# Three more input slots in the space of X2, a buffer of its own for the small spectra, and a smaller identity: one change to a fused recurrence and FFT-convolution kernel

## The chip, the cores and the metric

The kernel runs on one core of a Trainium2 chip. A core has four engines that compute: PE (matrix multiply, with its weight loads shown as PEld), DVE, ACT and POOL. SP issues the DMAs. Only PE writes to PSUM, and only DVE and ACT read it here. The metric is the device time of one execution in microseconds (us). Lower is better. For the kernel before, three executions gave 456.35, 457.14 and 457.5 us.

## The reference

The input x has 4 batches of 6272 time steps with 256 channels. First comes a gated linear recurrence, then a gated convolution over the whole sequence, computed with FFTs, between two projections.

```python
sig = 1.0 / (1.0 + np.exp(-f_logit))
f = lower_bound + (1.0 - lower_bound) * sig          # i = 1 - f
for t in range(S):
    h = f[:, t] * h + i[:, t] * x[:, t]
    y[:, t] = h
proj = y @ w_proj                                     # 256 -> 3 * 256: x1, x2, x3
X2 = np.fft.rfft(x2, n=S, axis=1)
H = np.fft.rfft(filter_fft, n=S, axis=0)
x2_conv = np.fft.irfft(X2 * H, n=S, axis=1)
out = (x1 * x2_conv * x3) @ w_out
```

## The kernel before

Every batch passes through the same phases.

- hgrn(b) computes the recurrence in 13 chunks of 512 steps (the last has 128). Of each chunk f_logit and x are loaded into a slot (FL and XT, L331). ACT takes the sigmoid in place (L334), POOL multiplies x by it (L336), and PE transposes both by 64x64 blocks against an identity matrix (L348, "su"). ACT or DVE makes f of it (L361, L363), and DVE runs the scan (L369), which writes h into HA. The two halves of the channels (kh) are done one after the other, so a chunk has two "su" and two scans. For the first six chunks there is also a copy behind the end of the sequence ("wrap").
- phase_p(b) projects h onto x2 by columns of HA with a step of 49 elements (98 matmuls with 256 columns, L703), and ACT or DVE moves the result from PSUM into X2 (L280, L285). It needs the whole scan of the batch.
- The spectrum runs in 16 units of 8 pairs. phase_f1 takes X2 as weights (L716), the result goes to A. "mini" and "zm" (L732, L737) multiply the real end frequencies of four units by the small spectra Hm and leave the products in zp. unit does the second step of the transform (L778), multiplies by the filter's spectrum H, which is loaded from DRAM again for most units (L756). That product is made by DVE straight from PSUM (L801), or by an evacuation to A and a product on POOL (L810). POOL adds the two halves of zp into PP ("slot", L783). I2 is the first step back (L820); its result goes to Th.
- gate(b) computes x1 times x3 in 13 chunks (L397 with L282, L287, L418, L427).
- phase_o(b) does the last step back (L883), multiplies by the gate on DVE (L889), projects by w_out (L901), evacuates and stores (L913).

In the prologue, the filter is loaded and transformed by the same two steps (L633, L651), the tables are made, and the H spectra are stored to DRAM. X2 serves there as a place for raw filter rows, and in batch 0 for three input slots more (more, slots0). Later the input has NX = 3 slots, which chunks take in turn by count["x"].

X2 holds, for each of 128 pairs, a row of PW = 116 elements: 49 columns, 15 of zeros, 49 columns, and 3 more of zeros. Hm, the small spectra, stands in 8 of those 15 columns of zeros (xv[:, :, Q:Q + 8]). "pad" (L665, L670) writes the zeros once, after the scan of batch 0.

What runs in which order is written by hand into a table, ORDER: for each operation its number, its engine and its PSUM bank. The operations are first declared with what they read and write (r, w), and the table is then issued in its sequence, so that every engine gets its instructions in this order and works them off one after the other. SP is a queue of this kind too: a load that waits for its slot holds up everything issued behind it. The operations of hgrn(b+1) stand in the table among those of the spectrum, gate(b) and phase_o(b).

Where an operation may run on either engine, the table chooses. "MUL" stands for a product made by DVE straight from PSUM.

Of the kernel before, what the change touches and what calls it, by code (L numbers as in the profile page):

```python
# [45 lines left out]
PW = 116  # L46
PF = 113
NX2 = 13
WR = 3072
# [12 lines left out]
class Plan:  # L62
# [63 lines left out]
    "A3gA7gAzgA/gAAYAOYAVIA0YA4AAhQAcQABIACIAPIASYAQAAWIAjQAaQAbQAdQAfQAgQAeQA5QA1SAoUBAYAiUA2KA8ABHgBfgBPgAlUBBUArWAnWBD"  # L126
    "gBLgBXgBTgBbgBjgA9WAsSA6ABIYBJSBCMBEYAyAARAAYUAwVDqgDrgDngAkVD2gECgADgD3gDpgEOgDogEDgEPgEagAqVBQIA+OAXIBFQAmVBRWAuVB"
    "SGApVBGAAZEBKKBYIAUIBMYBNSATYBUYAxVBZWBgABOKBaOAtVBVQBWABcIAvUBhWBiOBdUBkYBeEBlQBmIBpUBqMBwQBxIBnWBoODsAD4ADtYEEAB3U"
    "BuQBvIBrYAEYByYBsWBtOB4EDuSBzQB+UB0AB5WD5YDyQB/EB6GCAUEQACBEDvKDwKB7YEFYCCYB8SDzID0ID6WB9CCDUCEED+QCJSCQUD/AEcAEmgD7"
    "OD8OERYEbgCKKCRMCOWEAIEngEygEGSCHUCIMCPGEHCEIKEoAEdYCLYCSYEKWCTQELGCMUCUACNEEMOESSCZQETKCXWE0AEWUCaICYGCeQCgWEUKE8gE"  # L130
    "zgAFgE9gFGgFQgCGgEpYEJYCbYEXMEYME+ACfAChGCcSCdCEeQEiWEjGEfIEgICnUCoECpSEqUEkOAIACqCCjQCwSCuWErECiYE1YAJYCkAEsMEuQFIA"
    "CvGCsUCxKE2SCzWEvIEwICtEC+UC0GE3KE4KE5QCrYAHYAKYCyYC/EE/YE6ADAWE7IDBGC3UFASC5WFSAC4EDDQC6GFDUDEAC8WC9GEhYFHgFbgF6gFJ"
    "YCVgFRgCmgC7YFTYDCYFagCFgFkgFlgB2gFugCWgDGgFvgAGgFcAFBKFCKFKSDJQJTWJUXFEMFFMFLKDKAJWHJVODOUDPEFmAFMKDHQFNWDIAJYUFOOF"
    "POJaEFUSDQQFVCDRADMUFWKFXWFdYDNEFwAFnYDLYEtYALYDSYAMYEVYElYFxYDXQFYOFZOFeSDYADTUFfCFhQDUEDZWFgKFiADaGFjIFoUFpEDeSDfC"
    "DgWDhGFrQFySDcWFqMJZUJdVFzKF0KF1SFsAMugB1gC2gF4gGlgG3gF/gDWgClgDFgMigMWgF5gC1gMXgD1YEBYExYJXYANYDxYD9YDbYF7YF8YDiYFt"
    "IF2KF3KDdGDjWJbsJeQJiRENAEZAJfFGHSGTUJkBJgoDkOGVQGJWGWIGICMwAGUEGKOGXSGFQGZUGYCGGIGaEMkAGBWGRSGDUGSCGLQGNSGCOMYAGEMG"
    "MIGOKGPUGQEJjWJnXJoQJluJpHJqoGbUDmgDlgHAgMjgDVgGugGdSGhWGcEGeKGfQGmUJsSGiGGgAGosGqsF9WJuCJtTHTgHJQJxSJvrF+GGjUJzCGvW"
# [55 lines left out]
def kernel(  # L193
# [124 lines left out]
    def hgrn(b):  # L318
        for c in range(NCHK):
# [665 lines left out]
```

## Time and profile before

| | |
|---|---|
| median of 3 executions | 457.14 us |
| the profiled execution | 457.66 us, its span 455.5 us |
| PE busy | 436.8 us (96%) |
| DVE busy | 407.9 us (90%) |
| ACT busy | 392.8 us (86%) |
| POOL busy | 307.6 us (68%) |
| read from and written to HBM | 86.12 MB and 31.98 MB |

The span is the time from the first to the last record of the profiled execution. The busy time of PE counts matmuls whose ends are modelled, one overlapping the next, so a PE that is busy need not be at its peak. A row of a group gives line, engine, operation, output and inputs, shape, count, then the busy time in us and the mean duration of one in ns, and after the second bar the idle time of the engine ahead of these instructions with what ended it. A row of the chain of work gives its start and its length in us, and what the chain stood in. A row "A <- B: 31.7, 12, 12.5" of the waits says that A waited for B for 31.7 us in 12 times, and 12.5 us the longest time.

### The profile page before, as it was taken

What the parts mean: (1) busy time and instruction counts of PE and PEld (TensorE: products, weight loads), DVE (VectorE), ACT (ScalarE), POOL (GpSimd) and SP (SyncE); (2) the same over time, 40 slices, a digit from 0 to 9 for tenths busy, and PEclk for the clock granted to TensorE, in tenths of its full rate; (3) what the DMA queues carried; (4) which work ended last, traced back from release to release, by engine and by line L of the source; (5) the groups of instructions that cost most, each with busy time, mean ns of one, the idle gap of its engine ahead of it and who ended that gap; (6) DMA issues with size and microseconds to landing.
All of it is one profiled execution on the core that took longest, in us unless ns stands there. A gap on an engine that the chain in (4) does not pass through costs nothing.

```text
span 455.5 us, 14537 instructions
## 1 busy us (share of the span) xinstructions
PE 436.8 (96%) x6017; PEld 344.1 (76%) x6017; DVE 407.9 (90%) x456; ACT 392.8 (86%) x545; POOL 307.6 (68%) x287
## 2 busy tenths in 40 slices
PE   8999999999999999999999999999999899999994
PEld 6877778667767889767768988776769797776783
DVE  5889998899999986999999987999999859988973
ACT  5789998889999988999988978999999778998354
POOL 4588994289998642889986626999996505657300
PEclk9999999999999999999999999999999999999999
DMA  8999979767797977559956893589586822763167
GB/s 326 406 402 380 373 254 362 275 217 242 273 322 237 333 250 316 173 172 325 357 195 232 308 358 146 179 293 339 192 309 210 349 115 89 219 199 111 47 266 302
DMA packets 42562, 119.04 MB, mean 261 GB/s; under 512 B 4096, under 2 KB 5760, under 8 KB 42496
## 3 DMA queue, kind: packets, MB, share of 16 engines
q1 hardware_dynamic: 42496, 118.11, 72.7%
q8 instruction: 47, 0.77, 0.7%
q14 instruction: 19, 0.16, 0.1%
HBM read 86.12 MB, written 31.98 MB: 259 GB/s over the span
## 4 chain that ended last, share of the span: by engine, by line
PE 58%; DVE 14%; ACT 8%; issue 5%; DMA 5%; POOL 3%; SPq 0%; DVEq 0%; ACTq 0%; POOLq 0%
PE PS L397 14%; PE PS L820 8%; PE PS L703 7%; PE PS L901 7%; DVE HA L369 6%; PE PS L348 6%; PE PS L716 5%; PE PS L778 5%; DMA FL<-in_f_logit_dram 3%; PE PS L883 3%; DVE ys L889 3%; DMA XT<-in_x_dram 2%; DVE fTs L363 2%; PE PS L633 2%; DVE PP L801 2%
## 5 line engine op out<-in xcount | busy, mean ns | idle before, releaser
L336 POOL TENSOR_TENSOR XT<-XT,FL 128x1024 f32<-128x1024 f32 (+1 forms) x47 | 105.1, 2239 | 59.5 <-ACT FL L334 31.7
L369 DVE TENSOR_TENSOR_SCAN HA<-fTs,HA,PS 128x512 f16<-128x512 f32 (+1 forms) x96 | 112.8, 1204 | 3.0 <-ACT fTs L361 2.2
L397 PE MATMUL PS<-HA,W 128*128 128x490 f16 (+1 forms) x416 | 100.4, 367 | 0.3 <-ACT XS L282 0.2
L810 POOL TENSOR_TENSOR PP<-HA,Hu 98x1008 f16<-98x1008 f16 x43 | 90.2, 2106 | 4.3 <-ACT HA L280 2.0
L280 ACT CAST HA<-PS 128x1024 f16<-128x1024 f32 (+1 forms) x106 | 83.5, 821 | 4.9 <-PE PS L716 1.8
L889 DVE TENSOR_TENSOR ys<-PS,zt 128x1024 fp32r<-128x1024 f32 (+1 forms) x52 | 58.5, 1153 | 9.7 <-PE PS L883 5.4
L801 DVE TENSOR_TENSOR PP<-PS,Hu 98x1008 f16<-98x1008 f32 x53 | 62.2, 1199 | 1.5 <-PE PS L820 0.7
L901 PE MATMUL PS<-Wo,ys 128*128 128x256 f32 x392 | 57.8, 293 | 3.3 <-DVE ys L889 2.6
L361 ACT ACTIVATE fTs<-PS,nomc 128x512 f32<-128x512 f32 (+1 forms) x84 | 55.8, 673 | 4.7 <-PE PS L348 2.3
L397 PEld LDWEIGHTS <-W 128*128 128x128 f16 x416 | 35.2, 97 | 29.9 <-issue 3.3
L820 PEld LDWEIGHTS <-PP 98*128 98x128 f16 x1024 | 48.9, 98 | 11.3 <-issue 2.9
L418 DVE TENSOR_TENSOR zt<-PS,XS 128x490 f16<-128x490 f32 (+1 forms) x86 | 54.7, 653 | 2.3 <-DVE XS L287 0.5
L282 ACT ACTIVATE XS<-PS 128x490 f32<-128x490 f32 (+1 forms) x85 | 49.0, 584 | 8.7 <-DVE zt L418 5.1
L901 PEld LDWEIGHTS PS<-Wo,ys 128*128 128x128 f32 x392 | 49.5, 188 | 8.3 <-ACT PP L282 1.5
L280 ACT CAST Th<-PS 128x784 f16<-128x784 f32 x63 | 51.7, 823 | 4.0 <-PE PS L820 3.3
L820 PE MATMUL PS<-VA,PP 98*128 98x98 f16 x512 | 52.0, 207 | 0.8 <-POOL PP L783 0.3
L820 PE MATMUL PS<-VB,PP 98*128 98x98 f16 x512 | 51.8, 207 | 0.0
L334 ACT ACTIVATE FL<-FL 128x1024 f32<-128x1024 f32 (+1 forms) x47 | 47.4, 1012 | 3.0 <-DMA FL<-in_f_logit_dram 2.8
L703 PE MATMUL PS<-W,HA 128*128 128x256 f16 x392 | 43.8, 273 | 0.0
L703 PEld LDWEIGHTS <-HA 128*128 128x128 f16 x392 | 42.8, 142 | 0.7 <-ACT XS L282 0.3
L348 PE MATMUL PS<-iden,FL 64*128 64x64 f32 x704 | 40.3, 230 | 2.7 <-ACT osb L282 1.4
L348 PEld LDWEIGHTS PS<-iden,FL 64*128 64x128 f32 x704 | 30.2, 138 | 15.1 <-DVE HA L369 3.4
(112 smaller groups left out, 764.8 us busy)
## 6 DMA issues: line engine op xcount, KB each, us to landing
FL<-in_f_logit_dram SPq DMA_DIRECT2D x43, 512.0 KB, 5.9
XT<-in_x_dram SPq DMA_DIRECT2D x43, 512.0 KB, 6.7
Hu<-H SPq DMA_DIRECT2D x39, 512.0 KB, 4.4
out_dram<-osb SPq DMA_DIRECT2D x24, 512.0 KB, 4.6
out_dram<-PP SPq DMA_DIRECT2D x16, 512.0 KB, 5.2
Hl<-H SPq DMA_DIRECT2D x13, 512.0 KB, 4.5
out_dram<-HA SPq DMA_DIRECT2D x8, 512.0 KB, 6.1
X<-in_moe_filter_fft_dram SPq DMA_DIRECT2D x7, 512.0 KB, 6.2
```

The lines of the kernel that those rows point to most:

```text
L280: nc.scalar.copy(dst, src)
L336: op("u", {"POOL": 0.1 + 0.553 * nb}, lambda e, xt=xt, ft=ft: nc.gpsimd.tensor_tensor(xt, xt, ft, op=AOP.mult), r=[("ft", k)], w=[("xt", k)])
L348: nc.tensor.transpose(bank(pb)[:, at[p] + j:at[p] + hn:nb], src[ps, j, cols], iden[ps, ps])
L361: nc.scalar.activation(fT, sT, AF.Identity, scale=by, bias=1.0)
L369: nc.vector.tensor_tensor_scan(h, fT, bank(pb)[:, 512 - hn:512 + hn], init, op0=AOP.mult, op1=AOP.add),
L397: nc.tensor.matmul(PS[:, p, 0:n], W13[:, kh, js], HA[:, HB[kh] + t0:HB[kh] + t0 + n], start=(kh == 0), stop=(kh == 1))
L703: nc.tensor.matmul(pp[:, r - r0, :], column(HB[kh], q_of(r)), W2[:, kh, :], start=(kh == 0), stop=(kh == 1))
L801: nc.vector.tensor_tensor(pr, px.unsqueeze(1).broadcast_to([TB, 2, UE, 63]), hh(), op=AOP.mult)
L810: nc.gpsimd.tensor_tensor(pr, spec[:, o, :, 1:64].unsqueeze(1).broadcast_to([TB, 2, UE, 63]), hh(), op=AOP.mult)
L820: nc.tensor.matmul(PS[:, ib + o, pr * TB:(pr + 1) * TB], PP[:TB, k, o, n, 2 * pr:2 * pr + 2, :], v[:TB], start=(n == 0), stop=(n == 1))
L889: nc.vector.tensor_tensor(late["ys"][:, yk, :, 0:rn * 128], PS[:, cb:cb + 2, 0:rn * 128], late["zt"][:].rearrange("p k r m -> p k (r m)") ...
L901: nc.tensor.matmul(po[:, i, :], late["ys"][:, yk, kh, i * 128:(i + 1) * 128], Wo[:, kh, :], start=(kh == 0), stop=(kh == 1))
```

## The change

X2 is lent to the input again in batches 1 to 3. LENT names the chunks of a batch that use the three slots in X2; the others take the three normal slots in turn. lend() is an operation without an instruction that puts the borrowed use behind the last reader of X2 and the next use of X2 behind the borrowed one. Since the input overwrites the zeros, pads() writes them again after every scan (a memset of 15 columns in each row and one of the end, on POOL). Hm can no longer stand in the zeros and gets a buffer of its own, in which the 128 pairs lie side by side. The room for it comes from several places: rows of X2 are 113 elements and not 116, the tables FT, VA and VB lie in one buffer at a distance of 98 elements, zp has one buffer and not two, XS is shorter, and the identity that stays is [128, 64] (two 64x64 blocks one above the other). The full identity is f16 and lives only in the prologue. ORDER is new as a whole.

```diff
-PW = 116
+PW = 113
+LENT = ((), (5, 6, 7, 8, 9, 10), (5, 6, 7, 8, 9, 10), (7, 8, 9, 10))
...
-    iden = konst.tile([128, 128], F32, name="iden")
+    idc = konst.tile([128, 64], F32, name="idc")
...
-    FT = konst.tile([128, 2, 2, 128], F16, name="FT")
-    VA = konst.tile([128, TB], F16, name="VA")
-    VB = konst.tile([128, TB], F16, name="VB")
+    FTf = konst.tile([128, 6 * TB], F16, name="FT")
+    def FT(rows, o, r):
+        return FTf[rows, (2 * o + r) * TB:(2 * o + r) * TB + 128]
+    VA, VB = FTf[:, 4 * TB:5 * TB], FTf[:, 5 * TB:6 * TB]
...
-    Hm = xv[:, :, Q:Q + 8].rearrange("m i (e a k) -> m e a k i", e=2, a=2)
+    Hmt = konst.tile([128, 2, 2, 2, NEP], F16, name="Hm")
+    Hm = Hmt[:]
...
-    zp = konst.tile([128, 2, 2, 2, 2, NA * UE], F16, name="zp")
+    zp = konst.tile([128, 2, 2, 2, NA * UE], F16, name="zp")
...
+    count["x"] = 2
+    x2t = [("raw", i) for i in range(7)] + [("x2", g) for g in range(NX2)] + ["padX"]
+    x2t += [(t, NX + i) for t in ("ft", "xt") for i in range(3)]
+    def lend():
+        op("pre", {"SP": 0.01}, lambda e: None, w=x2t)
+    def pads():
+        op("pad", {"POOL": 2.0}, lambda e: nc.gpsimd.memset(xv[:, :, Q:64], 0.0), w=["padX"])
+        def tails(e):
+            nc.gpsimd.memset(X2[:, NEP * PW:], 0.0)
+        op("pad", {"POOL": 0.6}, tails, w=["padX"])
...
             if b == 0:
                 k = slots0[c]
+            elif c in LENT[b]:
+                k = NX + LENT[b].index(c) % 3
             else:
                 k = count["x"] % NX
...
-                                                    src[ps, j, cols], iden[ps, ps])
+                                                    src[ps, j, cols], idc[ps])
...
+        iden = tmp.tile([128, 128], F16, name="iden")
         op("iden", {"POOL": 0.6}, lambda e: make_identity(nc, iden), w=["iden"])
+        def corners(e):
+            for i in range(2):
+                at = slice(64 * i, 64 * i + 64)
+                dve.tensor_copy(idc[at], iden[at, at])
+        op("idc", {"DVE": 0.2}, corners, r=["iden"], w=["idc"])
...
-                e, xv[:TB, :, Q:Q + 8].rearrange("p i (e c) -> p i e c", e=2),
-                PS[:TB, pb:pb + 2].rearrange("p e (c i) -> p i e c", c=4), HS),
+                e, Hmt[:TB].rearrange("p e a k i -> p e (a k i)"), PS[:TB, pb:pb + 2], HS),
...
-        op("zm", {"DVE": 0.58}, prod, r=["Hm"], w=[("zp", q % 2)], src=mm)
+        op("zm", {"DVE": 0.58}, prod, r=["Hm"], w=["zp"], src=mm)
...
             if b + 1 < B:
                 plan.batch = b + 1
+                lend()
                 hgrn(b + 1)
+                lend()
+                pads()
```

More of the change, by code (lines that the diff above doesn't have):

```diff
@@ new lines @@
+    "ABMgBEgBJIAZWAsXAoXA9IA3MA+QBFIAaOAtXBKUAxXBGWAlSBQgArSBUgBYgBggBNYDqgBcgDogBkgBLEBRIA/IAUYBSSBOQBZYBHOAnUAvUAqUBVIB"
+    "TKBPADrgDsgD3gD4gAEgEDgDpgEEgEPgEbgEQgEngAyUBaUBbMBhYAuQBWQBXABiSBdIBjCAwUBeQBfIBlYBmSBnCBqQBrIDtADuYBxSBoUBpEByKBsY"
+    "BvQBwIBzYAFYD5AD6YB6SBtUB0QDvWB7CB4SBuMB5KB1ADwGCBUCCEDxOEFAB/QDzSD7UCAAB9WD0KD1KCEQCISEGYB8YCDYD8EB+GD9MCFAERAEdACJ"
+    "KD/WEAOCKQCLICRSCSCEpAEBOCPUEHQELSCQEEIICNWCOGCUUCVEESYEMKEJIENKEogETWEUGCMYEqYEzgCaQEcgEVOCbAEXUCYSCfQEYMEZMChWE9gE"
+    "0gE+gFIgAGgCTYEKYFRgE1ACZCEeYCcYCgACiOE2YE/ACjYCdSEfQEgIEhIFAYCeCCoUEjWCpECkSEkGClCErUCqQEvSEsECrAElOEwCEtMCxWCvQExK"
@@ new lines @@
+    "CyGCwIFTACtUE3WE4OE5OCuEC6SC0QAIYCsYC7CE6UC1AALYCzYAJYAKYAMYE7MDBSDCKE8MC/QFBWFHgFJAFbgB2gCGgFSgCXgFmgFlgFcgDAAFCGFD"
+    "OC4SFEQC5CDEUFFAC9SDFEC+CFGIFKYFLWEiYANYC8YEOYDDYFUYDIUDJEDKQFOSDLAFdADRUFMOFNODSEJSQJUADNWFVUDPQFwgFvgB3gFPKFQKFWMD"
+    "QIFXMJTSJXTDOGFnAFYWDUQEmYFeYDMYFoYD2YDTYCWgJZDJVCFxADVAFfSFgCDYUFZOFaOFiQDaWFhKDZEFjADbGFpUFqEDhSFkIFsWDdQDiCDfSFrM"
+    "FtGJYUJcVFuODGgF5gAHgCHgC3gCngMWgC2gCmgG2gDHgF+gGkgDeADgCEaIECYEyYFyYDcYAOYEuYJasJWYEWYFzQF2WF0ADyADkSJeFMYADlCF1IMX"
+    "gMugMigMvgDXgDngDmgG/gGtgDWgJdUJhQJiVD+YF3OF4OJjIGCWGUQGSSJfsGDOGEWJktGQUGRMGTCGVAGFGGISGJCMwAF6YDjYF7YMxYGGQGHIGAUM"
@@ new lines @@
+    "kAGBMGWSGYQGOWGXCGPGGZIGMUGNMGKSGLCJmWJnXJrUJtEGcSJoOJpvGaQGeUGgWGdKF8SGbAGhGGfMGlQGnoGiUJsWJwXF9CHISGjMJxQGpoGuUJuG"
+    "GysGwsJyHHJCJzAJqYJvYGvYGmYJ0YGxYGoYGqYGzYG3WHKSGrQG5uG7GHLCJ1VJ2XJ6SJ3FGsAJ4vG0UHAQHEoHCoG6YG8YG4YJ8CMZYHDYHBYHFYHO"
+    "SG1EHPCHMWJ7UJ/VJ9sG9SHTQHNGHQWKBFHVAG+CKAVKEUKFQHROHGWHcSKGEKHAHSgHXoKCtHHGHbgMjgHkgHtgHlQHpAHgqHeqH2UHfYHWYHhYHdYH"
+    "UYKIYIAgHYYHZWHnoHqYJgYH3EKJTKKRKLDHaGH4UKMpH5EHiSH6WHuQHjKHwoHyoH8UH7GH9EHoYHmYMlYHxYHrSIBWHsCHvYH+UKOQIFGH/MIDuKQA"
+    "IGYIEYHzYMaSMeUMbCIKQMfEMcKH0WMgMIOAH1GKPRIkSIJgIMoINYICYIHWITUISgIVsIbgKRBIlCIIGIXEMmSMqQMnCIcWMrIM6gM7gIugNGgMoKIg"
@@ new lines @@
+    "GIeGILYIPYJ5YKSYIWYIUYIYYMsIIQUIREKTXKUWKVHIoSIpCIZUIaEKYXKZQM8AKWuKaPKboIvSIzqIxqJbYIfYI0YIhYKDYImWInGKdRIqUKeQKiTK"
+    "fBKgoJlYIdYIiWIrEIjOKjSIsUItMM9YKcYNIAKkDKlqMVgI3gNHgMyQM2WJAgNSgNTgNfgF/gNegNogJJgNpgOQgMzAM0IM3GI4UI6EI8EKnTKoSKsU"
+    "KpDM+QKuEM4OKqqKtTKvrNJYM/ANUANAIKmYIwYI9YKXYIyYKxUNCWNDGNKSNEOKzENLCNMKI1QJBUJFsI7YI5YJ+YNVYJCYKNYI2AJDEJKWNOQI+SJO"
+    "GNPAI/CKyXK2UK3VK4ENgANQINWSNaQK0vNXCK5tK7XK8VLAUJMuNYKLBWNbAK9HK+tLCENqALDuJEYNcINhYJGYJNYK/YLFXLGUJLYK6YJPYKwYKhYL"
+    "EYLHHLIENiSNjCLKVJHWLLUNlQNygJIGLMFNkKNmAJQWLNsJRGLPVLQSR1ULZWLJYKrYNnILRFLUQLSqK1YLTYNrYR3ENsSNvUN0ANtCM5YNwENRYLOY"
@@ new lines @@
+    "MhYNdYLaOLbWLcGLVILWQLXANuKNxMLjSR2WR4GObgNzgN1YORgN9gN8gOGgNFYU6gN+AMdYN/YOHgU5gLYgOagLkKLeQN2UN5WN3EN6GLlSLmCLfILg"
+    "QN4MLtULhAN7OLuMOIALoSOAWODQOBGLvULpKLqSOJYOCOOEALwELrCOcAOFIOSAMpYOdYOTYM1YL3WL4OOKULySONQL5WOLELzKL0SOMML8ULdgLngL"
+    "igOkgOOAL6GL1COPIL9MOUWR6SOXQOVGR7TOWOL+UNBYOYAOZIR9DR8COeWOhSOfGOgOOlYOmYNNYMtYNZYLsgVFgOiCL/EVRgMGQMBWOjKOnSOtUMCO"
+    "MHIOoCO5WOrQOuMO/SOpUPAKO6GOqEO9WO+OOsAVHAOzSO1UO3WO2MO0CU7AO4GOvQOwIOxUO7SOyEVTAO8KMDQMLUMMMMAgVGgVSgL2gLxgPFSPBWME"
+    "AMFgL7gPHQPDUPGCPIIPCGPEEMISMQQPLWPJUMRIMJCPKMPTQPPuPNuPXAPVoPrSPsCMNUU8YVUYPOYVIYR5YPQYPUYPMYR/XSARPYYPWYPRSSBHMOEP"
@@ new lines @@
+    "bWSCpPSCPvUPjQPwEPduPfuPlAPZSPnoPcYPoYR+YPkYPgYPmYPeYPtUSEQPaCPuEPhWP1gP2SPxUPiGPyEP+gQHgSGIPpQP6qP4qMKgQQgSFWSJTSKX"
+    "PqASHuSLDSMHPzQP/UP0IQDsQBEU9SU+CQZQQaAP5YSNYQIWSOUSPVSQEP3YP7YQCYQAYQKGP8QQEYU/KSRtQMuVBSP9AQRUVCCVDKSTWQVESVGQFQSU"
+    "VQbWQTsSYSSaKSWtQGAQcGQdQSZTQfWSbrSdSQUYQLYQNYQWYQJYQSYSfKQeAQgGQOUQkQQhSQiKQjgQsgVdgQ+gQ1gQPEQooQmAVJWVKGQ2UQ4EQ6EQ"
+    "XSQtQQYCQxAVLOVNUSeWSiXRHSQvoVOMSguVPMQlYSDYQnYQuYSXYQwYQpYQyYVfASkHRICQqQSjXSnWSlvVVSQrASpGMSUMTERJQQzWQ/URKAVWKVXK"
+    "Q0GRNQROARBsRDsSoSRLWSsTSmYQ5YQ3YQ7YSqqREYRAYRCYVZQRMGSuDRPWRSUVegRQOVaAVbIVpgRagRRgVqgU4gV1gRjgQ8SRUsV2gWzgWBgW0gWM"
@@ new lines @@
+    "gRsgWCgRFWRWEStVSvtVgYQ9CRGGRbQRkSRfoVhWViOVjOVrARVYRTYRXYRoCRdARcYRYUSxTRmCSzDVlQRZESySS2TS3US7VS8WTAXVmAS0qVnIS4DS"
+    "5sS9FV3AS+uVsYVtSVxQVuCVvKTCHRgYTBUTFWTGXTKVShYS6YRnYScYRpYVyATHGTDsSrYRlYRqSTIvVzITMFRrCV4YTLUTPWTQVTNsV5SV9QTRGTSF"
+    "V6KV7KTOYReYSwYTUVTVUTZWTaXWDATWFTXsTTYRtSRhUV+AV/ITbGW9gWLgTcvWWgMPgMUgWVgTeWTfQTjRRxqRvCTgGThoS1YRyYRiEWEYWFWTlBWG"
+    "GTkSToTTpQTmqTtRRuYTiYRwYTJYTqDWHOTvBTroRzUR0ETuTTyRTzSTwrT0BT3UWIQT8WT1qTxYTsYTnYWNAaYSaZTVcYTEYTYYWXAWJASSYWOYVEYT"
+    "dYT2YS/YWYYSIYT4MVoYVYYVQYT9OWKIabDaaCT5UUBWWPSWSQUCOT6EWQCWRKUGUT+WWfgWggWpgUDSWqgdcgT7gWTAW1AT/GW/AWUIULWWZQUECUHM"
@@ new lines @@
+    "WaAWhAUMOWbIUIUWcWUQSUJEWdGURKWiYWrAWsYUVQV0YWAYVwYV8YUNUWeOUWIUOEUSSUTCUaWUbOWjUWmQWtSWkEWlMWnAUcWWoIdeAWuCUXUUAgW+"
+    "gUUgUKgUFgW2YVAYXAYVMYVkYUdGWvKUfQWwWUgIadSUYEWxGWyOafCW3UW6QW4EW5MW7AUhSW8IUiCXBWUkUXESXHgdogUZgUPgUjgUegdpgddgd0gX"
+    "CGXDOaeQUpWXFCagAXGKUlMUqOXaSXUQXcUXVAXbKXdEXKWXLOXiSXQQXgUXeWXRAXOQXfOXhEXjCdqAXSUUmSUnCXMWXNGd2AXPIXYQXTMXWSXZIXXC"
+    "UzWUuUUrQXIYdrYXJYdfYUvMU0OUsAXqSXkUXrKXoWXmQUwSXlEXuUXpOXnAXsQXwEXtIaiWajXanUacYahYUxCakOXysalvapEX2QdgSaoUasVatXax"
+    "WaqsX4AdhCX6AauFd1gUogYOQdiKavvXzYXxYXvYX3YX5YX7YdkUazGYPAX+SayXX0QdlMdmMYCCYAqa0HdsWX1AYGUdtGa2TYKEduOa4DX8Qa3VYIsa"
@@ L348, in turn @@
                                 nc.tensor.transpose(bank(pb)[:, at[p] + j:at[p] + hn:nb],
-                                                    src[ps, j, cols], iden[ps, ps])
-                su = op("su", {"PE": 0.126 * nb}, turn, r=[("ft", k), ("xt", k), "iden"], w=["qT"], take=2)
+                                                    src[ps, j, cols], idc[ps])
+                su = op("su", {"PE": 0.126 * nb}, turn, r=[("ft", k), ("xt", k), "idc"], w=["qT"], take=2)
                 j = count["f"] % 2
@@ L556, in prepare @@
         op("tabs", {"DVE": 0.5, "POOL": 0.8, "ACT": 0.6}, f_tables, r=["v", "masks"] + st, w=["FTr"])
-        op("ftz", {"POOL": 0.6, "DVE": 0.2}, lambda e: (dve if e == "DVE" else pool).memset(FT[:], 0.0), w=["FT"])
+        op("ftz", {"POOL": 0.6, "DVE": 0.2}, lambda e: (dve if e == "DVE" else pool).memset(FTf[:], 0.0), w=["FT", "VA", "VB"])
         def rest0(e):
-            copy(e, FT[:, 0, :, 0:98], t01, lowf)
+            copy(e, FTo(0), t01, lowf)
             copy(e, D1[:], w[:, 0:128])
@@ L564, in rest1 @@
         def rest1(e):
-            copy(e, FT[:, 1, :, 0:98], FT[:, 0, :, 0:98], odd)
+            copy(e, FTo(1), FTo(0), odd)
             copy(e, VA[:TB], tt[2][:TB], sgn[:TB])
@@ L573, in turn_cos @@
                     nc.tensor.matmul(PS[64 * x:64 * x + 64, p, i * 128:(i + 1) * 128],
-                                     w[:, i * 64:(i + 1) * 64], iden[:], start=True, stop=True)
-        it = op("idt", {"PE": 0.3}, turn_cos, r=["v", "iden"] + st, take=1)
+                                     D1[:, i * 64:(i + 1) * 64], iden[:], start=True, stop=True)
+        it = op("idt", {"PE": 0.3}, turn_cos, r=["D1", "iden"], take=1)
         op("idw", {"ACT": 0.6, "DVE": 0.6}, lambda e, p: copy(
@@ L582, in warm @@
         def warm(e, p, i):
-            half = iden[:].bitcast(F16)
+            two = iden[:].unsqueeze(1).broadcast_to([128, 2, 128])
             for k in range(4):
-                nc.tensor.matmul(PS[:, p, 0:256], half[:, 0:128], half, start=True, stop=True)
+                nc.tensor.matmul(PS[:, p, 0:256].rearrange("p (a n) -> p a n", a=2), iden[:], two, start=True, stop=True)
         for i in range(WARM):
@@ L664, in finish @@
         def finish():
-            op("pad", {"POOL": 2.0}, lambda e: nc.gpsimd.memset(
-                X2[:, 0:NEP * PW].rearrange("m (i c) -> m i c", c=PW)[:, :, Q:64], 0.0),
-               w=[("raw", i) for i in range(7)] + [("x2", g) for g in range(NX2)] + ["Hm"])
-            def tails(e):
-                nc.gpsimd.memset(xv[:, :, 113:PW], 0.0)
-                nc.gpsimd.memset(X2[:, NEP * PW:], 0.0)
-            op("pad", {"POOL": 0.6}, tails, w=[("raw", i) for i in range(7)] + [("x2", 1)])
+            pads()
             def last(e, pb):
@@ L681, in finish @@
             lst = op("last", {"PE": 0.6}, last, r=["mX", "FTr"], w=["FF2"], take=2)
-            op("hw", {"DVE": 1.15, "ACT": 0.95}, lambda e, pb: copy(
-                e, xv[:TB, :, Q:Q + 8].rearrange("p i (e c) -> p i e c", e=2),
-                PS[:TB, pb:pb + 2].rearrange("p e (c i) -> p i e c", c=4), HS),
+            op("hw", either(1024), lambda e, pb: copy(
+                e, Hmt[:TB].rearrange("p e a k i -> p e (a k i)"), PS[:TB, pb:pb + 2], HS),
                w=["Hm"], src=lst)
@@ L716, in mm @@
                 nc.tensor.matmul(pa[:, i, :], X2[:, j:j + 128], D1, start=True, stop=True)
-        f1 = op("F1", {"PE": 0.056 * UE}, mm, r=[("x2", g) for g in range(NX2)] + ["D1"], take=2)
+        f1 = op("F1", {"PE": 0.056 * UE}, mm, r=[("x2", g) for g in range(NX2)] + ["D1", "padX"], take=2)
         k = u % NA * UE
@@ L731, in mm @@
                     rows = slice(64 * e2, 64 * e2 + 64)
-                    nc.tensor.matmul(PS[:, pb + e2, k * n:k * n + n], FT[rows, 0, 0, :],
+                    nc.tensor.matmul(PS[:, pb + e2, k * n:k * n + n], FT(rows, 0, 0),
                                      A[rows, :, k, 0], start=True, stop=True)
@@ L779, in mm @@
                             PS[:, xb + e2, :].rearrange("p (i k) -> p i k", k=64)[:, :, ks],
-                            FT[rows, o, r, :], A[rows, ka:ka + UE, r, ks],
+                            FT(rows, o, r), A[rows, ka:ka + UE, r, ks],
                             start=(r == 0), stop=(r == 1))
@@ L924 @@
         hgrn(0)
-        for i, t in enumerate(more_t):
-            op("pre", {"SP": 0.01}, lambda e: None, w=t + [("ft", NX + i), ("xt", NX + i)])
+        lend()
         finish()
@@ L952 @@
                 plan.batch = b + 1
+                lend()
                 hgrn(b + 1)
+                lend()
+                pads()
         plan.emit()
```

100 lines of the change are left out of this document (31 added, 69 removed).

## The prediction

> **What bounds the kernel now.** I first read the busy line of the page, then cut the span at the places where the 98 matmuls of L703 begin (phase_p, once per batch, which needs the whole scan of its batch). The second fence is those four stretches. The columns are length, then busy time of PE, PE's weight loads, DVE, ACT and POOL, then clock, DMA share and GB/s.
>
> ```profile
> PE 436.8 (96%) x6017; PEld 344.1 (76%) x6017; DVE 407.9 (90%) x456; ACT 392.8 (86%) x545; POOL 307.6 (68%) x287
> ```
> ```profile
> 72.00:167.00 95.00, 92.36 (x1372) 72.05 (x1371) 91.27 (x95) 86.41 (x123) 69.26 (x60) 1.00 0.80 273
> 167.00:265.10 98.10, 96.57 (x1420) 76.87 (x1417) 91.52 (x97) 91.02 (x128) 73.33 (x60) 1.00 0.74 265
> 265.10:366.30 101.20, 97.90 (x1443) 77.80 (x1440) 93.82 (x99) 89.47 (x128) 75.97 (x61) 1.00 0.74 264
> 366.30:455.50 89.20, 81.63 (x1042) 63.86 (x1038) 68.04 (x77) 63.55 (x85) 32.65 (x31) 0.99 0.48 166
> ```
> So there is a prologue of 72 us, three periods of 95 to 101 us in which one batch's convolution runs beside the next batch's scan, and a last one without a scan. PE is nearly always busy, DVE hardly less. Inside the periods nothing is left to win:
>
> ```profile
> 96.00:140.00 44.00, 43.37 (x667) 30.54 (x667) 43.59 (x49) 42.54 (x66) 41.97 (x34) 1.00 0.79 271
> 188.00:240.00 52.00, 51.34 (x764) 37.19 (x762) 50.80 (x60) 48.76 (x75) 46.69 (x39) 1.00 0.76 266
> 286.00:340.00 54.00, 53.19 (x798) 38.49 (x797) 52.50 (x61) 50.92 (x79) 52.33 (x44) 1.00 0.77 268
> ```
> There PE and DVE both stand at 97 to 99%. What is idle lies at the ends of the periods, just ahead of L703 and, in the third, just behind it:
>
> ```profile
> 0.00:72.00 72.00, 68.37 (x752) 53.49 (x752) 63.24 (x90) 62.36 (x83) 56.41 (x76) 1.00 0.96 357
> 156.00:167.00 11.00, 9.93 (x181) 8.41 (x180) 10.32 (x11) 9.12 (x15) 7.58 (x11) 1.00 0.75 254
> 262.00:265.10 3.10, 2.42 (x44) 1.50 (x43) 2.89 (x4) 2.96 (x6) 2.87 (x6) 1.00 0.96 292
> 272.00:280.00 8.00, 7.49 (x89) 7.11 (x87) 5.31 (x7) 6.94 (x8) 2.67 (x2) 1.00 0.67 273
> 354.00:366.30 12.30, 10.37 (x174) 8.45 (x168) 10.76 (x12) 9.40 (x15) 5.46 (x7) 1.00 0.87 342
> ```
> PE is idle there for 1.07, 0.68, 0.51 and 1.93 us, together 4.19. The chain of work at these places (start, length, what) says why:
>
> ```profile
> 151.96 7.70 DMA XT<-in_x_dram
> 159.82 2.39 POOL XT L336
> 163.48 2.46 DVE HA L369 x2
> 265.47 8.79 DMA FL<-in_f_logit_dram
> 274.33 1.06 ACT FL L334
> 277.15 1.01 ACT X L280
> 349.79 7.08 DMA FL<-in_f_logit_dram
> 361.65 3.61 DVE HA L369 x3
> ```
> At 152 and 350 the chain stands in an input load that could not start earlier, since its slot was still being read; then come the sigmoid or product, the transposes, and the last scans. At 265 a load of the following batch is late, and its sigmoid on ACT holds up the evacuation of phase_p (L280) queued behind it. The SP queue shows the same from its side: it stood 110 us for the transposes to free a slot.
>
> ```profile
> SPq L331 <- PE PS L348: 110.0, 40, 10.0
> ```
>
> **The change part by part.** *Three more input slots.* From the end of batch b's F1 (the last reader of X2) to phase_p of b+1, chunks 5 to 10 (7 to 10 in the last) go to X2. The same 26 loads per batch are issued and no DMA is added. Since six chunks skip the ring of three, chunks 11 and 12 follow chunks 2 and 3 in their slots, and the next batch's chunk 0 follows chunk 4. The new order table uses it: counted in PE work issued, using the table's PE weights, the load of f for chunk 12 of batch 1 moves from 131 to 121, of batch 2 from 222 to 198, of batch 3 from 308 to 292 (390.8 in all); chunk 0 of batch 2 from 137 to 121, of batch 3 from 224 to 211. A load lands within about 9 us by the rows above, so these loads stop being the last thing to arrive. On PE the F1, I1 and proj operations stay where they were.
>
> What is late next is DVE: ahead of L703 it has the scans and the products of phase_o to do, and is idle for only 11.00-10.32 = 0.68, 3.10-2.89 = 0.21 and 12.30-10.76 = 1.54 us. L703 can't start earlier than DVE's work allows, so these 2.43 us are what the three starts gain; PE's own idle (1.07 + 0.68 + 1.93 = 3.68) is the upper end. The late sigmoid behind L703 is another matter, since DVE has slack there: 0.51 of PE. Sum: 2.94, upper end 4.19, lower end 0.
>
> *Waits added.* The lent loads wait for the last F1. In the SP queue stand the H loads and further input loads behind them; they are put where F1 has just ended, so I take 0. The pads (two memsets on POOL, formerly once) come after each scan, three times:
>
> ```profile
> L665 POOL MEMSET X<- 128x1920 f16 x1 | 1.7, 1704 | 0.0
> L671 POOL MEMSET X<- 128x16 f16 x1 | 0.1, 143 | 0.0
> L292 POOL COPY HA<-HA 128x512 f16<-128x512 f16 x46 | 27.0, 618 | 0.1
> ```
> That is 1.85 us of POOL per batch, 5.5 in all. A pad waits for the transposes of the last lent chunk; behind it on POOL stand three wrap copies in batch 1 (for which phase_p waits), the product of a chunk in batch 2, and nothing urgent in batch 3. F1 waits for the pad, with 10.87 us of L703 between. POOL is idle for 11.00-7.58 = 3.4 and 12.30-5.46 = 6.8 us at these places, so cost 0; without this cover 1.85 each.
>
> *Row pitch 116 to 113 in X2.* Weight loads of F1 (L716) now start at multiples of 226 bytes; a start at an odd element occurs in every second of 512. No row shows a contiguous f16 weight load from an odd element. The nearest are:
>
> ```profile
> 71.98 10.87 PE PS L703 x98
> 84.09 1.85 PE PS L716 x32
> L703 PEld LDWEIGHTS <-HA 128*128 128x128 f16 x392 | 42.8, 142 | 0.7 <-ACT XS L282 0.3
> L716 PEld LDWEIGHTS <-X 128*128 128x128 f16 x512 | 30.7, 98 | 8.7 <-issue 4.1
> L883 PE MATMUL PS<-ID,Th x784: 212/216/227, 142.5 to 447.7; 64*128 64x128 f16 x196
> ```
> Contiguous loads take 98 ns, loads of single elements 98 bytes apart 142. If odd starts were read like the latter, 256 loads would cost 44 ns more each, 11.3 us, all of it on PE, since F1 runs at 1.85/32 = 58 ns a matmul with little slack. The other end is 0: L883's moving operand starts at odd elements in half its cases, and all 784 lie within 212 to 227 ns. The new loads stay contiguous and are thus nearest to L716, so I take 0. The Trainium skill ("TensorE: Matmul & The Clock Gate", Weight-path perf modes) says that fast weight load reads 32 bits at a time, two f16; an odd start would break these pairs, and by that the 11.3 us would be paid. The same section gives as its condition only 128 weights of a type other than FP32, packed or strided; by that nothing is paid. L703's 142 against 98 shows that a strided load is not as fast, so the second reading doesn't hold to the letter here.
>
> The evacuation into X2 writes runs of four, no longer on 8 bytes. Rows:
>
> ```profile
> L280 ACT CAST X<-PS 128x1024 f16<-128x1024 f32 (+1 forms) x31 | 30.6, 1025 | 9.3 <-PE PS L703 9.1
> L285 DVE CAST X<-PS 128x1024 f16<-128x1024 f32 (+1 forms) x21 | 25.4, 1237 | 10.6 <-PE PS L703 9.7 <-DMA H<-PP 0.8
> L280 ACT CAST f<-PS 128x1024 fp32r<-128x1024 f32 x5 | 5.8, 1177 | 2.7 <-PE PS L618 2.7
> ```
> The filter's evacuation already has pitch 113 and costs 1177 on ACT, so between 0 and 152 ns each; both engines wait for L703 there, about 1 us at a time, so only the last one counts: 0 taken, 0.6 at most in four batches.
>
> *Small spectra in their own buffer, one zp.* The product of L737 reads Hm contiguously now: 0. With one zp, each zm but a batch's first (12) must wait until POOL's L783 has read the group before:
>
> ```profile
> POOL PP L783 <- DVE zp L737: 12.6, 5, 5.6
> L783 POOL TENSOR_TENSOR PP<-zp x64: 327/338/359, 90.7 to 424.9; 98x32 f16<-98x32 f16 x64
> L810 POOL TENSOR_TENSOR PP<-HA,Hu 98x1008 f16<-98x1008 f16 x43 | 90.2, 2106 | 4.3 <-ACT HA L280 2.0 <-PE PS L820 1.9 <-POOL XT L336 0.4
> L801 DVE TENSOR_TENSOR PP<-PS,Hu 98x1008 f16<-98x1008 f32 x53 | 62.2, 1199 | 1.5 <-PE PS L820 0.7 <-PE PS L778 0.4 <-ACT HA L280 0.3
> ```
> Before, 4 of these 12 stood ahead of the group's last L783 in the order, 8 behind it. Today POOL waits for DVE there (12.6 us), not the reverse. I take 0; bounds: 0 to one L810 (2.1 us) at each, 25 us.
>
> *Order table and prologue.* Engine choices shift a little. Outside phase_p and the prologue DVE loses two L801 and gains two 784-wide evacuations of Th among smaller ones, about -2 us in 380; three more X evacuations (3 x 1.24) go to DVE inside phase_p, where it waits anyway. Taken as 0, with -1.9 kept for the low end. The f16 identity, its 64-column copy (one small DVE operation), the wider table memset and the moved copies of the filter lie in the 72 us that the DMA fills (share 0.96): 0, within 1 us either way.
>
> **Sum.** The profiled run took 457.66 us (span 455.5). 457.66-2.94 = 454.7; it stood 0.52 above the median, so 454.2. What tells a change from none here is about 0.3%, 1.4 us.
>
> **Rivals.** (a) *The late chunk is only another one.* Chunks 8, 9, 10 again turn on three lent slots, each behind the transposes of the chunk three before; in batch 1 the product of chunk 10 is put at 129.0 of PE work against 129.4 before, with its transposes at 129.4 in both. Then the gap moves ahead and DVE idles there. For it: only chunks 11 and 12 gain much lead. Against it: DVE has 98% in that stretch today with the same spacing. Price: the 2.43 us are not gained, 457.14-0.5 = 456.6, 455.8 to 458.5.
> (b) *DVE waits for POOL at zm* (slower). For it: POOL is busy 52.33 of 54 us in the third period's middle. Against it: the direction of today's wait. It decides from 2.94/12 = 0.25 us at each; with half an L810 at half of the twelve, 6 x 1.05 = 6.3, 454.2+6.3 = 460.5.
> (c) *Odd weight starts are slow* (slower): 454.2+11.3 = 465.5.
> (d) *More is gained:* PE's whole idle (1.25 more) and DVE's 1.9: 451.0.
>
> **Chances.** Forecast 0.50 (452.3 to 455.7), (d) 0.12, (a) 0.17, (b) 0.13, (c) 0.08. Faster 0.62, same 0.17, slower 0.21. The range goes from (d) to (b)'s middle, 451.0 to 460.5, and leaves out half of (d), some of (b) and all of (c), 0.18.
>
> **What would show it.** Right: ahead of the second to fourth L703 no input load in the chain, DVE without a gap in the last 10 us, periods of about 94, 97 and 100 us; SP's wait for L348 well under 110. Wrong: L716 above 58 ns a matmul (c); DVE L737 waiting for POOL L783 (b); L336 of chunks 8 to 10 ended by a load (a); phase_p waiting for a pad.

## The result, and the profile after

The changed kernel takes 460.98 us (median of 6, 459.96 to 462.19) against 457.16 for the kernel before (median of 6). The ratio is 1.0087, 95% interval 1.0069 to 1.0104: slower by 0.9%, where 0.6% faster was forecast, and just outside the range.

Line numbers have moved. phase_p is L729 now, F1 L742, the evacuations L290 (ACT) and L295 (DVE), the scan L395, the load L357, zm L763, "slot" L809, the pad L336 and L339. In runs with a line more, numbers behind it are one higher (L730 for L729, L704 for L703). The columns of the stretches are those of the prediction. The busy line of the page, and the periods from one start of L729 to the next, of the changed kernel:

```profile
PE 438.5 (95%) x6013; PEld 344.0 (75%) x6013; DVE 411.0 (89%) x458; ACT 403.7 (88%) x549; POOL 314.8 (69%) x290
```
```profile
72.20:167.80 95.60, 92.21 (x1371) 71.72 (x1369) 89.75 (x92) 89.03 (x125) 72.81 (x63) 1.00 0.76 271
167.80:267.60 99.80, 97.36 (x1420) 76.29 (x1416) 92.91 (x98) 93.67 (x129) 74.63 (x60) 1.00 0.74 256
267.60:368.00 100.40, 98.95 (x1445) 78.01 (x1442) 94.09 (x100) 91.47 (x126) 80.56 (x65) 1.00 0.73 262
368.00:459.30 91.30, 82.64 (x1040) 64.73 (x1038) 69.80 (x77) 65.94 (x85) 31.75 (x31) 0.98 0.45 161
```
ACT is busy 10.9 us longer than before (392.8), PE only 1.7 (436.8). The last period, in which no input is loaded, is 2.1 us longer, so that loss isn't one of supply. I cut each period once more at the first matmul of F1. The four stretches from the first L729 to the first L742, with their sum, and the same for the kernel before (L703 to L716):

```profile
72.16:86.33 14.17, 12.77 (x105) 11.31 (x104) 10.77 (x10) 12.24 (x11) 3.49 (x4) 1.00 0.91 336
167.82:181.96 14.14, 12.77 (x126) 12.30 (x123) 11.02 (x8) 12.44 (x11) 2.38 (x1) 1.00 0.62 219
267.60:282.56 14.96, 14.39 (x139) 13.34 (x136) 12.04 (x10) 12.57 (x12) 4.81 (x3) 1.00 0.74 291
367.96:382.33 14.37, 13.04 (x114) 11.98 (x112) 9.17 (x7) 11.28 (x10) 0.00 (x0) 1.00 0.13 51
sum 57.64, PE 52.96 PEld 48.94 DVE 42.99 ACT 48.54 POOL 10.68; mean PE 13.24 PEld 12.24 DVE 10.75 ACT 12.13 POOL 2.67
```
```profile
71.97:84.00 12.03, 12.03 (x105) 11.15 (x104) 10.58 (x11) 9.55 (x11) 2.88 (x5) 1.00 1.01 380
167.02:179.38 12.36, 12.36 (x125) 12.13 (x123) 8.49 (x7) 10.91 (x13) 0.55 (x1) 1.00 0.93 358
265.10:279.25 14.15, 13.64 (x138) 13.22 (x135) 11.09 (x10) 10.40 (x11) 1.92 (x1) 1.00 0.88 338
366.31:378.34 12.03, 12.03 (x114) 11.78 (x111) 7.00 (x6) 9.11 (x11) 0.00 (x0) 1.00 0.16 61
sum 50.57, PE 50.06 PEld 48.28 DVE 37.16 ACT 39.97 POOL 5.34; mean PE 12.51 PEld 12.07 DVE 9.29 ACT 9.99 POOL 1.34
```
These stretches have grown by 57.64 - 50.57 = 7.1 us. PE, which never waited in three of the four before, now stands idle for 57.64 - 52.96 = 4.7 us. ACT's busy time in them grew by 48.54 - 39.97 = 8.6 us. The other stretches (from F1 to the next L729, or to the end) shrank by 3.4 us, and the prologue grew by 0.2; together +3.8, the difference of the two spans (459.3 and 455.5). So there is a gain of about the size forecast, and a loss twice as large.

The groups of the evacuation name the loss (by shape, first the changed kernel, then the kernel before):

```profile
L290 ACT CAST X<-PS 128x1024 f16<-128x1024 f32 x28 | 38.8, 1479 | 8.5 <-PE PS L729 8.5
L295 DVE CAST X<-PS 128x1024 f16<-128x1024 f32 x20 | 28.9, 1468 | 10.5 <-PE PS L729 10.4
```
```profile
L280 ACT CAST X<-PS 128x1024 f16<-128x1024 f32 x30 | 29.3, 1015 | 9.2 <-PE PS L703 9.1
L285 DVE CAST X<-PS 128x1024 f16<-128x1024 f32 x18 | 21.5, 1221 | 9.3 <-PE PS L703 8.4 <-DMA H<-PP 0.8
```
Moving the same 1024 elements into X2 takes 464 ns longer on ACT and 247 on DVE. The chain of work in the last of these stretches runs through it (changed kernel):

```profile
371.32 1.50 ACT X L290
375.48 5.40 ACT X L290 x4
382.35 1.70 PE PS L742 x28
```

### The profile page after: what moved, and what is told of

It reads as the page before. It is cut to its first block, busy times and chain, and to the rows that moved or that the text cites. A ratio compares the mean times of both kernels' runs of the same rounds, so it can differ in the third digit from the quotient of the medians.

```text
span 459.3 us, 14538 instructions
## 1 busy us (share of the span) xinstructions
PE 438.5 (95%) x6013; PEld 344.0 (75%) x6013; DVE 411.0 (89%) x458; ACT 403.7 (88%) x549; POOL 314.8 (69%) x290
## 4 chain that ended last, share of the span: by engine, by line
PE 58%; DVE 15%; ACT 11%; issue 6%; POOL 4%; DMA 4%; SPq 1%; ACTq 0%; DVEq 0%; POOLq 0%
PE PS L423 15%; PE PS L846 9%; DVE HA L395 7%; PE PS L927 7%; PE PS L742 6%; PE PS L804 6%; PE PS L374 5%; ACT X L290 5%; PE PS L729 4%; DVE ys L915 3%; PE PS L909 3%; DMA out_dram<-osb 2%; DMA X<-in_moe_filter_fft_dram 2%; PE PS L666 1%; POOL PP L836 1%
## 5 line engine op out<-in xcount | busy, mean ns | idle before, releaser
L395 DVE TENSOR_TENSOR_SCAN HA<-fTs,HA,PS 128x512 f16<-128x512 f32 (+1 forms) x96 | 112.8, 1202 | 1.8 <-ACT fTs L387 0.8
L423 PE MATMUL PS<-HA,W 128*128 128x490 f16 (+1 forms) x416 | 101.6, 368 | 0.9 <-DVE zt L444 0.3
L836 POOL TENSOR_TENSOR PP<-HA,Hu 98x1008 f16<-98x1008 f16 x44 | 92.2, 2105 | 8.4 <-ACT HA L290 4.2
L362 POOL TENSOR_TENSOR XT<-XT,FL 128x1024 f32<-128x1024 f32 (+1 forms) x31 | 67.0, 2165 | 38.4 <-ACT FL L360 38.4
L290 ACT CAST HA<-PS 128x1024 f16<-128x1024 f32 (+1 forms) x107 | 84.0, 817 | 5.3 <-PE PS L742 1.7
L846 PEld LDWEIGHTS <-PP 98*128 98x128 f16 x1024 | 50.0, 97 | 9.5 <-issue 2.2
L362 POOL TENSOR_TENSOR X<-X 128x1024 f32<-128x1024 f32 x21 | 50.0, 2380 | 9.7 <-ACT X L360 7.4
L846 PE MATMUL PS<-FT,PP 98*128 98x98 f16 x1024 | 55.7, 206 | 0.5 <-DVE HA L395 0.5
L290 ACT CAST Th<-PS 128x784 f16<-128x784 f32 x61 | 49.9, 821 | 3.1 <-PE PS L846 2.6
L729 PE MATMUL PS<-W,HA 128*128 128x256 f16 x392 | 45.5, 273 | 2.3 <-ACT X L290 2.2
L290 ACT CAST X<-PS 128x1024 f16<-128x1024 f32 (+1 forms) x29 | 40.0, 1475 | 8.5 <-PE PS L729 8.5
L729 PEld LDWEIGHTS <-HA 128*128 128x128 f16 x392 | 43.2, 142 | 4.1 <-issue 3.3
L453 POOL TENSOR_TENSOR zt<-XS 128x490 f16<-128x490 f32 x18 | 22.0, 1228 | 32.1 <-DVE ys L915 19.1
L295 DVE CAST X<-PS 128x1024 f16<-128x1024 f32 (+1 forms) x23 | 32.8, 1453 | 10.7 <-PE PS L729 10.6
```

The source lines that it names most:

```text
L290: nc.scalar.copy(dst, src)
L362: op("u", {"POOL": 0.1 + 0.553 * nb}, lambda e, xt=xt, ft=ft: nc.gpsimd.tensor_tensor(xt, xt, ft, op=AOP.mult), r=[("ft", k)], w=[("xt", k)])
L395: nc.vector.tensor_tensor_scan(h, fT, bank(pb)[:, 512 - hn:512 + hn], init, op0=AOP.mult, op1=AOP.add),
L423: nc.tensor.matmul(PS[:, p, 0:n], W13[:, kh, js], HA[:, HB[kh] + t0:HB[kh] + t0 + n], start=(kh == 0), stop=(kh == 1))
L729: nc.tensor.matmul(pp[:, r - r0, :], column(HB[kh], q_of(r)), W2[:, kh, :], start=(kh == 0), stop=(kh == 1))
L836: nc.gpsimd.tensor_tensor(pr, spec[:, o, :, 1:64].unsqueeze(1).broadcast_to([TB, 2, UE, 63]), hh(), op=AOP.mult)
```

## The experiments

Two theories stood. **P**: the row pitch of 113 elements makes these evacuations slow. **R**: the borrowed slots or the new order do. Everything was measured beside the kernel before on the same chip.

**The pitch alone**, in the kernel before:

```diff
-PW = 116
+PW = 113
...
-                nc.gpsimd.memset(xv[:, :, 113:PW], 0.0)
+                if PW > 113:
+                    nc.gpsimd.memset(xv[:, :, 113:PW], 0.0)
```


> The kernel before with nothing changed but the row pitch of X2, 116 to 113 elements (its memset of columns 113 to 115 falls away). Theory P (the pitch makes the evacuations into X2 slow, and phase_p becomes bound by them): evacuations into X2 at about 1475 ns on ACT and 1453 on DVE, as in the changed kernel, from L703 to the first F1 about 14.2 us instead of 12.0, in all 6 to 7 us longer: about 463.5. Rival R (the evacuations are slow because of the borrowed slots, whose input loads write X2, or because of the new order): evacuations stay at 1025 and 1237, the time at 457.2 within 0.5.

Measured: 462.92 against 456.49, ratio 1.0136 (95% interval 1.0092 to 1.0179). The evacuations, in the kernel before with pitch 113:

```profile
L280 ACT CAST X<-PS 128x1024 f16<-128x1024 f32 x30 | 41.6, 1474 | 5.2 <-PE PS L704 4.1 <-DVE X L285 1.1
L285 DVE CAST X<-PS 128x1024 f16<-128x1024 f32 x18 | 25.4, 1469 | 9.6 <-PE PS L704 8.8 <-DMA H<-PP 0.8
```
The durations of the changed kernel appear with no borrowed slot and the old order. R falls.

**The change with another pitch.** Wider rows of X2 need more room. It came from x3s (the second factor of the gate), kept in f16; its effect alone is the first of these three runs.

```diff
-    XS = konst.tile([128, 4 * XR * Q], F32, name="XS")
+    XS = konst.tile([128, 2 * XR * Q], F32, name="XS")
+    X3 = konst.tile([128, 2 * XR * Q], F16, name="X3")
```


> The changed kernel with only the second factor of the gate (x3s) kept in f16 instead of f32, which frees 1960 bytes per partition for the runs beside it. Both theories: as the changed kernel, 461.0 within 0.6; evacuations into X2 still at about 1475 and 1453 ns.

Measured: 460.32, ratio 1.0082 (1.0057 to 1.0107), as expected: the room it gives costs and brings nothing that matters here.

```diff
-PW = 113
+PW = 114
...
         def tails(e):
+            nc.gpsimd.memset(xv[:, :, 113:PW], 0.0)
             nc.gpsimd.memset(X2[:, NEP * PW:], 0.0)
```


> The changed kernel (x3s in f16) with X2 at 114 elements a row (228 bytes): every row starts on 4 bytes, every second one not on 8. Columns 113 to 115 stay zero by one more memset after each scan. Theory P in the form that a 4-byte word is the unit: as fast as at 116, evacuations near 1025 and 1237, about 454. Theory P in the form that 8 bytes or 16 bytes are the unit: runs of 8 bytes cross a boundary in 1/2 (8) or 1/4 (16) of the cases instead of 3/4 or 3/8, so two thirds of the loss stay: evacuations near 1325 and 1380, about 458.7. Rival R: 461.

Measured: 452.85, ratio 0.9929 (0.9897 to 0.9961).

> The changed kernel (x3s in f16) with X2 at the old 116 elements a row (232 bytes, every row on 8 bytes), all else of the change kept, one more memset after each scan. Theory P: evacuations back at 1025 and 1237, L703 to first F1 back at 12.0 us, and the gain of the earlier loads shows: 461.0 - 7.1 = 453.9, faster than the kernel before. Rival R: evacuations stay slow, about 461.

Measured: 452.61, ratio 0.9913 (0.9884 to 0.9943). Faster than both kernels, with all of the change but its pitch (and x3s in f16). The evacuations at 114, then at 116:

```profile
L290 ACT CAST X<-PS 128x1024 f16<-128x1024 f32 x28 | 27.7, 1050 | 11.3 <-PE PS L730 11.3
L295 DVE CAST X<-PS 128x1024 f16<-128x1024 f32 x20 | 24.1, 1221 | 10.5 <-PE PS L730 10.4
```
```profile
L290 ACT CAST X<-PS 128x1024 f16<-128x1024 f32 x28 | 27.1, 1021 | 11.5 <-PE PS L730 11.5
L295 DVE CAST X<-PS 128x1024 f16<-128x1024 f32 x20 | 24.1, 1221 | 10.5 <-PE PS L730 10.3
```
One element more per row takes the whole loss away. At 114 half of the runs of four still cross an 8-byte boundary and a quarter a 16-byte one, and that costs 29 ns on ACT and nothing on DVE; the forms of P with these units, which wanted two thirds of the loss to stay, fall. What is left is the start inside a 4-byte word, which at 113 every second row has.

**Odd starts without the pitch.** Rows of 116, and X2 begins one element later:

```diff
-    xv = X2[:, 0:NEP * PW].rearrange("m (i c) -> m i c", c=PW)
+    xv = X2[:, 1:1 + NEP * PW].rearrange("m (i c) -> m i c", c=PW)
...
-                j = (u * UE + i) * PW
+                j = (u * UE + i) * PW + 1
```


> As a_pitch116 (all of the change but the pitch, 452.6), but X2 begins one element later, so that every run of four that is written into X2, and every weight load of F1, starts on an odd element; in the changed kernel that holds for every second row. Theory W (a run of f16 that starts inside a 4-byte word costs extra in ACT and DVE, whatever the pitch): the extra doubles against the changed kernel, from 450 to about 900 ns on ACT and from 216 to 432 on DVE, so 1925 and 1669 ns per evacuation, L703 to first F1 at 16 us or more, in all 464 to 468. Rival L (the pitch of 226 bytes is the cause, by the lines or boundaries that its rows cross, not the odd start): evacuations near those of a_pitch116, 1025 and 1237, time 452.6. For F1's weight loads both expect no change: 98 ns, 56 ns from one matmul to the next.

Measured: 472.34 against 456.30, ratio 1.0347 (1.0331 to 1.0363). The groups of this kernel:

```profile
L290 ACT CAST X<-PS 128x1024 f16<-128x1024 f32 x28 | 50.3, 1926 | 8.1 <-PE PS L730 8.1
L295 DVE CAST X<-PS 128x1024 f16<-128x1024 f32 x20 | 37.3, 1904 | 11.3 <-PE PS L730 11.1
L743 PEld LDWEIGHTS <-X 128*128 128x128 f16 x512 | 32.2, 101 | 10.7 <-issue 5.2 <-POOL XT L363 0.9
```
ACT's extra doubles as theory W said (1926 forecast as 1925): 905 ns for 256 runs, 3.5 ns for each that starts odd. DVE's extra grows by more than twice, from 247 to 683, which no theory had; that this kernel is later than W's 464 to 468 goes with it. F1's weight loads, all of them odd here, take 101 ns instead of 98.

**Is the gain that of the early loads?** The next kernel is a_pitch116 with some operations of the table moved: the loads, sigmoids and products of chunks 11 and 12 of batches 1 to 3 and the loads of chunk 0 of batches 2 and 3. Counted in PE work issued, with the table's weights, they stand again where the kernel before has them, or up to 1 us later. One is only half put back: the load of f for chunk 0 of batch 3 stands at 219, between the 211 of the change and the 224 of before.

> As a_pitch116, but in the order table the loads, sigmoids and products of chunks 11 and 12 of batches 1 to 3 and the loads of chunk 0 of batches 2 and 3 are put back to where the kernel before has them, in PE work issued; the lent slots and all else stay. Theory S (the gain of 4 us at 116 comes from these loads being early): L703 of batches 2 to 4 starts later again, 2.4 to 4 us of the gain go, 455 to 456.6. Rival T (the gain comes from the cheaper product of the small spectra and from the new engine choices): 452.6 within 0.8.

Measured: 456.54, ratio 1.0003 (0.9991 to 1.0016): 3.9 us go, as much as the whole gain, but not in the places where it was won. The stretches from the first F1 to the next L703 or L730, in us:

| kernel | to the second | to the third | to the fourth |
|---|---|---|---|
| before | 83.02 | 85.72 | 87.06 |
| a_pitch116 | 80.72 | 85.35 | 85.43 |
| a_late | 80.75 | 87.2 | 86.9 |

The chain ahead of the third (first two lines) and fourth L730 (last line), with the late loads:

```profile
255.94 5.51 DMA XT<-in_x_dram
262.41 0.74 POOL XT L363
362.90 0.73 POOL XT L363
```
With the early loads (a_pitch116) it is the scan that stands there:

```profile
258.24 3.63 DVE HA L396 x3
356.12 4.80 DVE HA L396 x4
```
Ahead of the fourth, the late loads give back what was won. Ahead of the third they cost 1.5 us more than was ever won: an input load stands in the chain, which had none there in the kernel before, and by the tables chunk 12 has less time than it had (its load of f at 222.7 of PE work and its transposes at 223.7, before at 222.2 and 224.1). Ahead of the second nothing changes, but the supply isn't put back there. The loads stand late in the table, yet their data are there earlier than in the kernel before: POOL begins the product of chunk 11 at 156.94 us with the late loads, at 157.42 with the early and at 159.82 in the kernel before. So this run doesn't show where the 2.3 us of that stretch come from. One further run put all chunks from 5 on back:

> As a_late, but the loads, sigmoids and products of all chunks from 5 on (and the loads of the next batch's chunk 0) in batches 1 to 3 stand where the kernel before has them, in PE work issued. a_late gave back the gain of batches 2 and 3, but from the first F1 of batch 0 to L703 of batch 1 it still took 80.75 us (before 83.02). Theory S (that gain too comes from early loads, those of the lent chunks 5 to 10): 82 to 83 us there, in all 457.5 to 459. Rival T (it comes from other choices of the order table and the cheaper product of the small spectra): 80.7 to 81 us there, in all 456.5 within 0.7.

Measured: 474.55, ratio 1.0371 (1.0322 to 1.0421), with 90.3 us from the first F1 to the second L730, far beyond either theory. Over the whole run DVE's scans wait 16.1 us for f from ACT (2.2 in the kernel before), so this table isn't the old supply but a worse one, and the run doesn't tell the two theories apart. What won the first period's 2.3 us stays open. Two things differ there between the kernel before and a_pitch116: the product of chunk 11 starts 2.4 us earlier, and DVE has less to do (78.91 us busy, before 80.71; three products of the gate fewer stand in the stretch, and zm is shorter). No run parts them.

**Two smaller parts**, both against a_pitch116:

```diff
-    Hmt = konst.tile([128, 2, 2, 2, NEP], F16, name="Hm")
+    Hmt = konst.tile([128, NEP, 2, 2, 2], F16, name="Hm")
```


> As a_pitch116, but the small spectra lie in their own buffer with the eight values of a pair side by side, so that zm reads them in steps of 16 bytes (before: 232 bytes) instead of contiguously. Theory S: zm goes from 419 to about 600 ns as before the change, 16 times 0.18 = 2.9 us of DVE in all, of which less than a third shows: 452.6 to 453.6. Rival T: most of the 2.9 us shows, 454.5 to 455.5.

Measured: 453.98, ratio 0.9944 (0.9931 to 0.9956), zm at 613 ns instead of 420: 1.4 of the 3.1 us of DVE show, between the two theories.

```diff
-    VA, VB = FTf[:, 4 * TB:5 * TB], FTf[:, 5 * TB:6 * TB]
+    VA, VB = FTf[:, 4 * TB:5 * TB], FTf[:, 5 * TB + 6:6 * TB + 6]
```


> As a_pitch116, but the table VB starts 992 bytes into its buffer, on 16 bytes, instead of 980. In the changed kernel, a group of 16 matmuls of I2 takes 667 ns from its first to its last start, against 652 before. If the start of VB is the cause: back to about 652, 64 groups times 15 ns = 1 us, about 451.7. If it isn't: 452.6, groups at 667.

Measured: 452.43, ratio 0.9913 (0.9899 to 0.9926). The groups of I2 go back from 667 to 652 ns, so the start of the table is the cause of that; the time moves by 0.2, no more than noise. 1 us less on PE is not 1 us less in all.

## Why the prediction was wrong

- **The step that failed is the evacuation into X2**, "between 0 and 152 ns each", "0 taken, 0.6 at most in four batches". It cost 464 ns on ACT and 247 on DVE, and 7.1 us of time in the changed kernel (6.4 for the pitch alone). It went wrong twice. The upper bound was taken from the filter's evacuation, which has the same pitch in elements; but its elements have 4 bytes, and no run of it can start inside a 4-byte word. And the cover ("about 1 us at a time, so only the last one counts") did not hold: in the changed kernel both engines still wait for L729, 8.5 and 10.4 us, about as long as before (9.1 and 8.4), so these waits did not take up the extra. ACT alone had 28 x 0.464 = 13.0 us more to do, more than all its waits. The order table fixes which engine takes which evacuation: in the last of the four stretches ACT takes six in a row without a gap, 374.16 to 382.18 us, while DVE waits 3.6 us for L729. PE waits for ACT's evacuations there now.
- **The odd start was weighed at the wrong place.** The text spent its rival (c) on F1's weight loads. Their row is unchanged at 98 ns (30.9 us for 512), and with every start odd they take 101. Of the two readings of the Trainium skill ("TensorE: Matmul & The Clock Gate", Weight-path perf modes), the one by which an odd start breaks the pairs of a 32-bit read falls; for packed loads the trace agrees with the one that only asks for 128 weights that are not FP32 (98 and 101 ns). The 142 ns of L703's strided loads stay outside it.
- **The gain was right in part.** 2.94 us were forecast; at pitch 116 it is 3.9 (452.61 against 456.49), but 1.4 of these are the small spectra's. Ahead of the third and fourth L703, 0.21 and 1.54 us were forecast and 0.4 and 1.6 won; behind the third, 0.51 and 0.58 (a_pitch116: PE busy for 13.57 of 13.57 us, 13.64 of 14.15 before). The input loads left the chain, so rival (a) falls. That the early loads are the cause is shown for the fourth alone, where putting them back gives 1.5 us back. Ahead of the second, 2.3 us were won where 0.68 was the cap by DVE's idle time, for a reason not found; that the sum comes near the forecast is partly luck. One sign failed: SP's wait for the transposes was to be well under 110 us and is 104.0 in the changed kernel, 105.3 at pitch 116, though the loads had left the chain.
- **Small spectra: 0 was wrong by 1.4 us.** The contiguous read makes zm 420 ns instead of 608 (16 of them). No row of before showed it, and the text gave no bound.
- **zp in one buffer: right.** DVE's L763 waits for PE (2.9 us), not for POOL, and POOL still waits for it. The new table puts all twelve behind the last L809 of the group before (8 of 12 in the old one). Rival (b) falls:

```profile
POOL PP L809 <- DVE zp L763: 7.8, 3, 3.0
DVE zp L763 <- PE PS L758: 2.9, 5, 0.9
```
- **Pads: right, 0.** Four memsets of 1823 ns (1704 before: they too write odd starts), and nothing waited for them. The margin is small: in a_late the pads and the copies behind them stand in the chain ahead of the second L730, where PE waits 0.2 us for the copies.

```profile
L336 POOL MEMSET X<- 128x1920 f16 x4 | 7.3, 1823 | 0.7 <-PE PS L374 0.7
```
- **The range** ended at 460.5, the middle of (b). The cost that came was in none of the cases, since its bound was set too low.
- **A slip without effect:** not three but two more evacuations of 1024 elements into X2 went to DVE (20, before 18).

## What to carry to other kernels

When an edit changes where 16-bit rows start, look at every instruction that writes them in short runs, and bound it from rows with the same element size and the same parity of start; a row with 4-byte elements says nothing on that. A cover has to be summed for each engine by itself: the extra of all its instructions in the stretch against its own waits, and a wait that stays where it is covers nothing. A change that seems to lose may be a gain and a loss: cut the span at the same events in both kernels, and see each stretch by itself before judging the whole.

## What the runs showed of the hardware

- A run of four f16 written from PSUM into SBUF costs ACT 3.5 ns more when it starts inside a 4-byte word: 1021 ns for 256 runs with none odd, 1479 with half, 1926 with all. Short runs alone cost nothing: the same 1024 elements into the contiguous buffer of F1's result take 1022 on ACT and 1220 on DVE (a_pitch116). On DVE, with none, half and all odd, it is 1221, 1468 and 1904, so the first half costs 247 and the second 436; why is open. The Trainium skill ("SBUF — State Buffer", Operand start alignment) has such starts as legal for f16 and says that its runs timed nothing; here they are timed.
- A weight load of 128 f16 from an odd element costs 3 ns of about 100.
- A group of 16 matmuls of I2 (98 columns, L846) takes 667 and not 652 ns from first to last start when the table VB, the moving operand of every second one, starts 980 and not 992 bytes into its buffer.
